# A fused sliding-attention and mixture-of-experts kernel: values of key blocks accumulated unsplit in two overlapping parts, loads moved, two router steps rewritten

## The chip, the cores and the metric

The kernel runs on one core of one Trainium2 chip. The metric is device time in microseconds (us) of one execution. A core has five engines that run side by side and wait for each other through semaphores: TensorE (PE in the profile; PEld is its weight load), VectorE (DVE), ScalarE (ACT), GpSimd (POOL) and SyncE (SP, which here only starts DMAs). Each engine runs its own instructions in program order. Matmuls write into PSUM, which VectorE and ScalarE read.

## What is computed

First causal attention with a window of 128 positions and a linear distance bias, then a router that gives each token to one of eight experts:

```
q, k, v: (8, 8, 576, 64)            # batch, heads, positions, head dimension
scores = q @ k.T / sqrt(64) - slope[h] * |i - j|,  kept where 0 <= i - j < 128
attn   = exp(scores - max); attn /= sum(attn)
x      = (attn @ v) as (4608 tokens, 512)
logits = x @ w_gate                  # (4608, 8)
e(t)   = argmax(logits); gate = softmax(logits)[e(t)]
out[t] = gate * (relu(x[t] @ w1[e(t)]) @ w2[e(t)])     # 512 -> 1024 -> 512
```

All is in float32.

## The kernel before

**Attention in 16 units.** A unit is a pair of batches and a pair of heads (four pairs of batches `bp`, four pairs of heads `hp`). Its 576 keys are nine blocks `kb` of 64 (`KB`). Key block `kb` is seen by 192 queries, from query 64·kb on (128 for block 7, 64 for block 8). A unit has four steps g = 0 to 3, one for a group of key blocks: (0, 1), (2, 3), (4, 5), (6, 7, 8). A step does, in this order, which is written out by hand in the loop at L1173:

- `load_unit` (L612): DMAs for k, q and half of v on SP, and for the other half of v on POOL, two units ahead;
- `scores(i + 2)` (L732): matmuls of keys and queries for the group two steps ahead (L739), the exponential on ScalarE (L745), and the multiplication with the bias and the mask on VectorE (L748, L753) into a tile `pe`;
- `values` (L762): matmuls of `pe` and `v` into the PSUM tile `at` (L774). Four 64x64 matmuls (two batches `c`, two heads `r`) occupy the four quadrants of the array at the same time;
- `finish` (L782) after a half of the queries: the eviction of `at` into `xT` on ScalarE (L791, L793), the sums of `pe` over keys by matmuls with a column of ones (L806) into a PSUM tile `m`, and their eviction into `sumT` (ScalarE L815 for the first head pair, else an addition on VectorE L817);
- `some()` (L1161): one entry of a list `tasks`, the router's work for the pair of batches before (`behind`, L1143).

The queries are cut into two halves (`QH`, L577): 0 to 319 and 320 to 575. Key blocks 3 and 4 are seen from both halves, so their matmuls are split. `at` is one tile of two PSUM banks with one buffer; each half uses it afresh. The PSUM tiles `m` share a pool of two buffers, for the sums and for all the router's matmuls.

**The router's tasks** are, by name: `gate`, `turn` (matmuls and turns of the logits), `scale_a` and `scale_b` (VectorE: the denominators, the logits summed over heads at L882, the best expert), `scale_c`, `count`, `place` (a token's place in its expert's list), `ones_at` (one-hot matrices `oc`, nine instructions at L955, and `orow`, L960), `enlist` (matmuls of both, L970), and `row` (a token tile turned by four matmuls, L984, evicted by ScalarE, L986, and written to memory). For batch pairs 0 to 2 they run in the steps of the next units; for the last pair they run as `with_tail` (L1426) between the matmuls of the first expert (L1273, L1330).

**Experts.** From about 190 us on TensorE runs eight experts, each with gathered rows (L1090) and scattered results (L1353).

The step that the change touches, for g = 2 and 3 (L1195 to L1204):

```
            elif g == 2:
                values(u, 0, (4,))
                finish(u, 0)
                values(u, 1, (3, 4, 5))
            else:
                values(u, 1, (6, 7, 8))
                finish(u, 1)
            ...
            some()
```

Of the kernel before, what the change touches and what calls it, by code (L numbers as in the profile page):

```python
# [457 lines left out]
def kernel(  # L458
# [12 lines left out]
    nc = tc.nc  # L471

    Dm, N = qT.shape
    D = Dm // H
    E = moe_w_gate.shape[1]
# [5 lines left out]
    KB = P // 2  # L481
    NK = S // KB
    BP = N // S // 2
    TPB = 2 * S // P
# [7 lines left out]
    NS = NJ + NF  # L492
# [13 lines left out]
    with ExitStack() as fast:  # L506
        def pool(stack, name, bufs, **kw):
            return stack.enter_context(tc.tile_pool(name=name, bufs=bufs, **kw))
# [65 lines left out]
              [(6, 0, 192), (7, 192, 128), (8, 320, 64)]]  # L574
        GC = 384
        LQ = 4 * P
        QH = [(0, 5 * KB), (5 * KB, 4 * KB)]  # L577

        ac = pool(att, "att_consts", 1)
        qk = pool(att, "qk", 3)  # L580
# [3 lines left out]
        ps_a = pool(att, "ps_a", 1, space=PSUM)  # L584
# [4 lines left out]
        units = [(bp, hp) for bp in range(BP) for hp in range(HP)]  # L589
# [58 lines left out]
        fac = ac.tile([P, H, GC], F32, name="fac")  # L648
# [8 lines left out]
        ind = ac.tile([P, HP, 32], F32, name="ind")  # L657
# [4 lines left out]
        none = ac.tile([P, 32], F32, name="none")  # L662
# [27 lines left out]
        K = {}  # L690
# [38 lines left out]
        prob, xT, sumT, gs = {}, {}, {}, {}  # L729
        at = {}  # L730
# [25 lines left out]
        def block(u, kb):  # L756

            g = min(kb // 2, 3)
            c0, n = next((c, n) for k, c, n in GR[g] if k == kb)
            return prob[4 * u + g], c0, n  # L760

        def values(u, half, kbs):  # L762

            bp, hp = units[u]
            q0, qn = QH[half]
            if (u, half) not in at:
                at[u, half] = ps_a.tile([P, 2, 512], F32, name="at"), set()
            acc, begun = at[u, half]
            for kb in kbs:
                pe, c0, n = block(u, kb)  # L770
                lo, hi = max(q0, kb * KB), min(q0 + qn, kb * KB + n)
                for c in range(2):
                    for r in range(2):
                        nc.tensor.matmul(  # L774
                            acc[r * D : (r + 1) * D, c, lo - q0 : hi - q0],
                            lhsT=v_sb[u][c * KB : (c + 1) * KB, kb, r * D : (r + 1) * D],
                            rhs=pe[c * KB : (c + 1) * KB, r, c0 + lo - kb * KB : c0 + hi - kb * KB],
                            start=(c, r) not in begun, stop=True, skip_group_check=True,
                        )
                        begun.add((c, r))  # L780

        def finish(u, half):  # L782

            bp, hp = units[u]
            q0, qn = QH[half]
            if hp == 0 and half == 0:
                xT[bp] = xp.tile([P, HP, 2 * S], F32, name="xT")
                sumT[bp] = xp.tile([P, S], F32, name="sumT")
            acc = at.pop((u, half))[0]
            n = min(q0 + qn, LQ) - q0  # L790
            nc.scalar.copy(xT[bp][:, hp, : 2 * LQ].rearrange("p (b q) -> p b q", b=2)[:, :, q0 : q0 + n], acc[:, :, :n])  # L791
# [3 lines left out]
            ops = []  # L795
            for kb in range(max(0, q0 // KB - 2), (q0 + qn) // KB):
                pe, c0, n = block(u, kb)
                lo, hi = max(q0, kb * KB), min(q0 + qn, kb * KB + n)
                ops.append((kb % 2, lo, hi, pe, c0 - kb * KB))
            if half == 0:  # L800
                ops.insert(0, (1, 0, KB, None, 0))
            begun = set()
            for par, lo, hi, pe, off in ops:
                for r in range(2):
                    j = 2 * r + par
                    nc.tensor.matmul(  # L806
                        sm[32 * j : 32 * j + 32, lo - q0 : hi - q0],
                        lhsT=none[:] if pe is None else ind[:, hp, :],
                        rhs=fac[:, 0, :KB] if pe is None else pe[:, r, off + lo : off + hi],
                        start=j not in begun, stop=True, skip_group_check=True,  # L810
                    )
                    begun.add(j)
            to = sumT[bp][:, q0 : q0 + qn]
            if hp == 0:
                nc.scalar.copy(to, sm[:, :qn])  # L815
            else:
                nc.vector.tensor_tensor(to, sm[:, :qn], to, op=ALU.add)  # L817


        def gate(bp, c):  # L820
# [58 lines left out]

        def scale_b(bp):  # L880
            lg = small.tile([P, TPB, E], F32, name="lg")
            nc.vector.reduce_sum(lg[:], pr_of[bp].rearrange("p t a h e -> p t e (a h)"), axis=AX)  # L882
# [67 lines left out]
        def ones_at(bp):  # L950

            rc = slot_of[bp]
            oc = small.tile([P, TPB, E * NS], F32, name="oc")
            for t in range(TPB):
                nc.vector.tensor_scalar(  # L955
                    oc[:, t, :], K["cols"][:, : E * NS], scalar1=rc[:, 1, t : t + 1],
                    scalar2=K["tok"][:, bp * TPB + t : bp * TPB + t + 1], op0=ALU.is_equal, op1=ALU.mult,
                )
            orow = small.tile([P, TPB, P], F32, name="orow")
            nc.vector.tensor_tensor(  # L960
                orow[:], K["cols"][:, None, :].to_broadcast([P, TPB, P]),
                rc[:, 0, :].unsqueeze(2).to_broadcast([P, TPB, P]), op=ALU.is_equal,
            )
            oh_of[bp] = oc, orow
# [196 lines left out]
        def some():  # L1161
            if tasks:
                for f in tasks.pop(0):
                    f()
# [8 lines left out]
        for i in range(NG):  # L1173
            u, g = divmod(i, 4)
            bp, hp = units[u]
            if g == (0 if u else 2) and u + 2 < len(units):
                load_unit(u + 2)
            if g == 0:
                if u == 5:
                    load_w1(fixed[0], w1_a)  # L1180
                if u == 1:
                    token_numbers()
                if u == 3:
                    table_consts()
            if i + AHEAD < NG:
                scores(i + AHEAD)
            if 8 <= u < 12 and g % 2 == 1:
                ws_tasks.pop(0)()
            if g == 0:
                values(u, 0, (0, 1))  # L1190
                if u < HP - 1:
                    factors(u + 1)
            elif g == 1:
                values(u, 0, (2, 3))
            elif g == 2:  # L1195
                values(u, 0, (4,))
# [250 lines left out]
        for i in range(len(groups)):  # L1447
            g = groups[i]
# [65 lines left out]
```

## Time and profile before

| | |
|---|---|
| median of 6 runs | 720.49 us (718.09 to 722.1) |
| the profiled execution | 719.96 us, of which its span from the first to the last instruction 718.1 us |
| TensorE busy | 682.4 us, 95% of the span |
| VectorE, ScalarE, GpSimd busy | 346.0, 225.4 and 136.4 us |
| granted TensorE clock, mean | 0.99 |

Matmuls are pipelined and their ends are modelled, so TensorE's busy share does not say that it runs at its peak. A row of the timeline holds: start in us, duration in us, engine, line, operation, tiles written and read, shape, count, and in brackets the idle time of the engine before it with what ended it. Every float32 matmul of the program appears as two records.

### The profile page before, as it was taken

The numbers are of one execution on the slowest core, as the hardware profiler recorded it, in microseconds if no ns is written. First come the engines' busy times: TensorE is split into PE (matmuls) and PEld (weight loads), VectorE is DVE, ScalarE is ACT, GpSimd is POOL, SyncE is SP. The second block draws the span as 40 slices with busy tenths as digits, with TensorE's granted clock in tenths as the row PEclk, the third lists the DMA queues.
The fourth block names the chain that finished last, engine by engine and source line by source line (L and its number), as shares of the span: only waits on it lengthen the run. The fifth ranks groups of instructions, "written<-read, shape, count | busy, mean of one in ns | idle before, by whom it ended". The sixth has DMA issues, their size and how long they took to land.

```text
span 718.1 us, 14588 instructions
## 1 busy us (share of the span) xinstructions
PE 682.4 (95%) x6204; PEld 568.9 (79%) x6204; DVE 346.0 (48%) x671; ACT 225.4 (31%) x410; POOL 136.4 (19%) x222
## 2 busy tenths in 40 slices
PE   5799999989899999999999999999999999999994
PEld 4587778667587888878897888888788978878892
DVE  3356748775558574433542535255145534433410
ACT  4455556454343223203311320232133023203200
POOL 4320133411100250023022002301220230021020
PEclk9999999999998999999999999999999999999998
DMA  9967885783515862185338236731843582184010
GB/s 253 242 203 247 238 239 182 206 224 98 175 72 185 293 241 66 53 291 209 118 94 314 89 118 210 283 118 36 291 171 118 170 307 76 57 290 150 1 59 8
DMA packets 52092, 122.00 MB, mean 170 GB/s; under 512 B 3680, under 2 KB 14528, under 8 KB 52017
## 3 DMA queue, kind: packets, MB, share of 16 engines
q1 hardware_dynamic: 43120, 95.66, 40.7%
q0 software_dynamic: 7744, 24.43, 10.3%
q8 instruction: 51, 0.84, 0.5%
q10 hardware_dynamic: 1152, 0.88, 0.4%
q14 instruction: 25, 0.20, 0.1%
HBM read 101.79 MB, written 19.96 MB: 170 GB/s over the span
## 4 chain that ended last, share of the span: by engine, by line
issue 57%; PE 21%; POOL 11%; DVE 4%; ACT 3%; DMA 3%; another core or an unknown queue 0%; POOLq 0%; DVEq 0%
PE sp L739 5%; POOL out_dram L1353 5%; PE at L774 5%; POOL xg L1090 5%; PE m L984 2%; PE m L806 2%; DMA v_sb<-in_v_dram 2%; PE m L970 1%; PE pair0b L1273 1%; ACT pe L745 1%; PE m L826 1%; ACT xT L791 1%; DMA out_dram<-zo,s_idx 1%; DVE pe L748 1%; DVE oc L955 1%
## 5 line engine op out<-in xcount | busy, mean ns | idle before, releaser
L1353 POOL DMA_INDIRECT out_dram<-zo,s_idx x39 | 43.9, 1125 | 384.5 <-DVE zo L1344 283.7
L774 PE MATMUL at<-pe,v_sb 64*64 64x192 f32 (+2 forms) x1408 | 63.0, 287 | 10.0 <-ACT xT L791 7.0
L748 DVE TENSOR_TENSOR pe<-pe,fac 128x768 f32<-128x768 f32 x48 | 46.1, 960 | 47.0 <-ACT pe L745 47.0
L739 PE MATMUL sp<-q_sb,k_sb 64*64 64x192 f32 (+2 forms) x1152 | 60.6, 322 | 8.1 <-DMA q_sb<-in_qT_dram 7.2
L745 ACT ACTIVATE pe<-sp 128x768 f32<-128x768 f32 x64 | 51.9, 812 | 50.9 <-PE sp L739 45.9
L774 PEld LDWEIGHTS at<-pe,v_sb 64*64 64x64 f32 x1408 | 47.8, 136 | 17.0 <-ACT xT L791 9.2
L739 PEld LDWEIGHTS sp<-q_sb,k_sb 64*64 64x64 f32 x1152 | 41.9, 137 | 20.4 <-issue 9.1
L1090 POOL DMA_INDIRECT xg<-x_rows,g_idx x39 | 42.9, 1101 | 31.5 <-DVE tb L1013 14.4
L1108 ACT COPY xgT<-m 128x512 f32<-128x512 f32 x39 | 22.9, 586 | 36.4 <-PE m L1107 35.4
L806 PE MATMUL m<-pe,ind 128*32 128x192 f32 (+2 forms) x704 | 30.4, 288 | 3.8 <-issue 3.4
L1284 ACT ACTIVATE h<-h 128x512 f32<-128x512 f32 x32 | 20.2, 630 | 40.3 <-DVE h L1283 35.1
L986 ACT COPY xs<-m 128x512 f32<-128x512 f32 x36 | 20.4, 585 | 31.9 <-PE m L984 17.0
L501 DVE TENSOR_TENSOR xn<-xg 128x512 f32<-128x512 f32 x39 | 26.1, 685 | 7.7 <-PE m L1107 7.7
L990 POOL COPY xs<-ext 128x16 f32<-128x16 f32 x36 | 13.8, 396 | 78.5 <-DVE ext L909 31.9
L806 PEld LDWEIGHTS m<-pe,ind 128*32 128x32 f32 x704 | 23.5, 110 | 6.6 <-issue 4.0
L608 POOL DMA_DIRECT2D v_sb<-in_v_dram x15 | 11.2, 747 | 77.3 <-PE at L774 75.6
L1107 PE MATMUL m<-ident,xn 128*128 128x128 f32 x156 | 23.5, 274 | 0.7 <-DVE xn L501 0.7
L1107 PEld LDWEIGHTS m<-ident,xn 128*128 128x128 f32 x156 | 19.2, 141 | 4.9 <-PE m L1107 0.9
L984 PE MATMUL m<-ident,xT 128*128 128x128 f32 x144 | 21.6, 281 | 0.5 <-DVE hole L1021 0.5
L1385 PE MATMUL pair2a<-w,h 128*128 128x512 f32 x48 | 21.1, 592 | 0.0
L753 DVE TENSOR_TENSOR pe<-pe,fac 128x768 f32<-128x768 f32 x16 | 15.2, 951 | 8.9 <-ACT pe L745 8.8
L791 ACT COPY xT<-at 128x640 f32<-128x640 f32 (+1 forms) x32 | 18.6, 581 | 2.2 <-PE m L806 1.3
(357 smaller groups left out, 1395.8 us busy)
## 6 DMA issues: line engine op xcount, KB each, us to landing
w<-in_moe_w_dram SPq DMA_DIRECT2D x30, 2048.0 KB, 10.0
k_sb<-in_kT_dram SPq DMA_DIRECT2D x15, 576.0 KB, 6.9
q_sb<-in_qT_dram SPq DMA_DIRECT2D x15, 576.0 KB, 7.8
x_rows<-xs SPq DMA_DIRECT2D x32, 264.0 KB, 2.9
v_sb<-in_v_dram SPq DMA_DIRECT2D x15, 288.0 KB, 6.8
v_sb<-in_v_dram POOLq DMA_DIRECT2D x15, 288.0 KB
x_rows<-xs SPq DMA_DIRECT2D x8, 132.0 KB, 2.4
xg<-x_rows,g_idx POOLq DMA_INDIRECT x39
```

The lines of the kernel that those rows point to most:

```text
L501: nc.vector.tensor_tensor(to.rearrange("p (h d) -> p h d", h=H), rows[:, :Dm].rearrange("p (h d) -> p h d", h=H), rows[:, Dm : Dm + H].uns ...
L739: nc.tensor.matmul(sp[c * KB : (c + 1) * KB, r, c0 : c0 + n], lhsT=k_sb[u][hs, c, kb * KB : (kb + 1) * KB], rhs=q_sb[u][hs, c, kb * KB : k ...
L745: nc.scalar.activation(pe[:], sp[:, :, :GC], AF.Exp, scale=SCALE)
L748: nc.vector.tensor_tensor(pe.rearrange("p r (k c) -> p r k c", k=2), pe.rearrange("p r (k c) -> p r k c", k=2), fac[:, h0 : h0 + 2, None, ...
L774: nc.tensor.matmul(acc[r * D : (r + 1) * D, c, lo - q0 : hi - q0], lhsT=v_sb[u][c * KB : (c + 1) * KB, kb, r * D : (r + 1) * D], rhs=pe[c ...
L791: nc.scalar.copy(xT[bp][:, hp, : 2 * LQ].rearrange("p (b q) -> p b q", b=2)[:, :, q0 : q0 + n], acc[:, :, :n])
L806: nc.tensor.matmul(sm[32 * j : 32 * j + 32, lo - q0 : hi - q0], lhsT=none[:] if pe is None else ind[:, hp, :], rhs=fac[:, 0, :KB] if pe is ...
L984: nc.tensor.transpose(ps[:, hp * P : (hp + 1) * P], xT[bp][:, hp, t * P : (t + 1) * P], ident[:])
L1090: nc.gpsimd.indirect_dma_start(out=g["xg"][:, j, :], out_offset=None, in_=src, in_offset=bass.IndirectOffsetOnAxis(ap=g_idx[:, g["c0"] + j ...
L1107: nc.tensor.transpose(tp[:, db * P : (db + 1) * P], xn[:, db * P : (db + 1) * P], ident[:])
L1108: nc.scalar.copy(g["xT"][:, :, j * P : (j + 1) * P], tp.rearrange("p (d q) -> p d q", d=DB))
L1353: ins = nc.gpsimd.indirect_dma_start(out=out[:, :], out_offset=bass.IndirectOffsetOnAxis(ap=s_idx[:, g["c0"] + j : g["c0"] + j + 1], axis= ...
```

## The change

Values: the two parts of the queries now overlap. Part 0 takes key blocks 0 to 4 whole (queries 0 to 447), part 1 key blocks 5 to 8 (queries 320 to 575). Queries 320 to 447 get a share from each: ScalarE evicts part 0 as it is, and VectorE adds part 1's share to it when it reads part 1. `at` becomes two tiles of one bank each, one for each batch. The sums are cut in the same way. The matmuls of key block 5 go behind `some()`.

Loads: units 2 and 3 (the third and the fourth) are loaded from unit 1's steps 0 and 2 instead of unit 0's step 2 and unit 1's step 0. Router: the logits' sum over eight heads is made by three additions instead of one reduction, and `oc` by two instructions over nine tiles instead of nine. Core of the diff:

```diff
-        QH = [(0, 5 * KB), (5 * KB, 4 * KB)]
+        QH = [(0, 5, 0, 7 * KB), (5, 4, 5 * KB, 4 * KB)]
...
 # values
-                at[u, half] = ps_a.tile([P, 2, 512], F32, name="at"), set()
+                at[u, half] = [ps_a.tile([P, 512], F32, name=f"at{c}") for c in range(2)], set()
...
-                lo, hi = max(q0, kb * KB), min(q0 + qn, kb * KB + n)
+                lo = kb * KB - q0
...
 # finish
-            n = min(q0 + qn, LQ) - q0
-            nc.scalar.copy(xT[bp][:, hp, : 2 * LQ].rearrange("p (b q) -> p b q", b=2)[:, :, q0 : q0 + n], acc[:, :, :n])
-            if n < qn:
-                nc.scalar.copy(xT[bp][:, hp, 2 * LQ :].rearrange("p (b q) -> p b q", b=2), acc[:, :, n:qn])
+            both = QH[1][2]
+            seen = QH[0][3]
+            for c in range(2):
+                x = xT[bp][:, hp, c * LQ : (c + 1) * LQ]
+                if half == 0:
+                    nc.scalar.copy(x[:, :seen], acc[c][:, :seen])
+                else:
+                    nc.vector.tensor_tensor(x[:, both:seen], acc[c][:, : seen - both], x[:, both:seen], op=ALU.add)
+                    nc.scalar.copy(x[:, seen:], acc[c][:, seen - both : LQ - both])
+                    nc.scalar.copy(xT[bp][:, hp, 2 * LQ + c * KB : 2 * LQ + (c + 1) * KB], acc[c][:, LQ - both : qn])
...
+            if half == 0:
+                add_up(
+                    1, lambda s: s.rearrange("p (a c) -> p a c", c=KB)[:, 0:7:6, :], none[:],
+                    lambda r: fac[:, r, : 2 * KB].rearrange("p (a c) -> p a c", c=KB),
+                )
+            else:
+                add_up(0, lambda s: s[:, :KB], none[:], lambda r: fac[:, r, :KB])
+            for kb in range(kb0, kb0 + kbn):
+                pe, c0, n = block(u, kb)
+                lo = kb * KB - q0
+                add_up(kb % 2, lambda s: s[:, lo : lo + n], ind[:, hp, :], lambda r: pe[:, r, c0 : c0 + n])
...
-            if hp == 0:
-                nc.scalar.copy(to, sm[:, :qn])
-            else:
-                nc.vector.tensor_tensor(to, sm[:, :qn], to, op=ALU.add)
+            add = qn if hp else (seen - both if half else 0)
+            if add:
+                nc.vector.tensor_tensor(to[:, :add], sm[:, :add], to[:, :add], op=ALU.add)
+            if add < qn:
+                nc.scalar.copy(to[:, add:], sm[:, add:qn])
...
 # scale_b
-            nc.vector.reduce_sum(lg[:], pr_of[bp].rearrange("p t a h e -> p t e (a h)"), axis=AX)
+            pr = pr_of[bp]
+            ph = pr[:, :, 0, :, :]
+            nc.vector.tensor_tensor(ph, ph, pr[:, :, 1, :, :], op=ALU.add)
+            nc.vector.tensor_tensor(ph[:, :, 0:2, :], ph[:, :, 0:2, :], ph[:, :, 2:4, :], op=ALU.add)
+            nc.vector.tensor_tensor(lg[:], ph[:, :, 0, :], ph[:, :, 1, :], op=ALU.add)
...
 # ones_at
-            for t in range(TPB):
-                nc.vector.tensor_scalar(
-                    oc[:, t, :], K["cols"][:, : E * NS], scalar1=rc[:, 1, t : t + 1],
-                    scalar2=K["tok"][:, bp * TPB + t : bp * TPB + t + 1], op0=ALU.is_equal, op1=ALU.mult,
-                )
+            nc.vector.tensor_tensor(
+                oc[:], K["cols"][:, None, : E * NS].to_broadcast([P, TPB, E * NS]),
+                rc[:, 1, :].unsqueeze(2).to_broadcast([P, TPB, E * NS]), op=ALU.is_equal,
+            )
+            nc.vector.tensor_tensor(
+                oc[:], oc[:],
+                K["tok"][:, bp * TPB : (bp + 1) * TPB].unsqueeze(2).to_broadcast([P, TPB, E * NS]), op=ALU.mult,
+            )
...
 # the loop over steps
-            if g == (0 if u else 2) and u + 2 < len(units):
+            if g == 0 and u == 1:
+                load_unit(2)
+            if g == (2 if u == 1 else 0) and 0 < u < len(units) - 2:
                 load_unit(u + 2)
...
                 values(u, 0, (4,))
                 finish(u, 0)
-                values(u, 1, (3, 4, 5))
...
             some()
+            if g == 2:
+                values(u, 1, (5,))
```

More of the change, by code (lines that the diff above doesn't have):

```diff
@@ L764, in values @@
             bp, hp = units[u]
-            q0, qn = QH[half]
+            q0 = QH[half][2]
             if (u, half) not in at:
-                at[u, half] = ps_a.tile([P, 2, 512], F32, name="at"), set()
+                at[u, half] = [ps_a.tile([P, 512], F32, name=f"at{c}") for c in range(2)], set()
             acc, begun = at[u, half]
@@ L774, in values @@
                         nc.tensor.matmul(
-                            acc[r * D : (r + 1) * D, c, lo - q0 : hi - q0],
+                            acc[c][r * D : (r + 1) * D, lo : lo + n],
                             lhsT=v_sb[u][c * KB : (c + 1) * KB, kb, r * D : (r + 1) * D],
-                            rhs=pe[c * KB : (c + 1) * KB, r, c0 + lo - kb * KB : c0 + hi - kb * KB],
+                            rhs=pe[c * KB : (c + 1) * KB, r, c0 : c0 + n],
                             start=(c, r) not in begun, stop=True, skip_group_check=True,
@@ L784, in finish @@
             bp, hp = units[u]
-            q0, qn = QH[half]
+            kb0, kbn, q0, qn = QH[half]
             if hp == 0 and half == 0:
@@ L789, in finish, with add_up @@
             acc = at.pop((u, half))[0]
-            n = min(q0 + qn, LQ) - q0
-            nc.scalar.copy(xT[bp][:, hp, : 2 * LQ].rearrange("p (b q) -> p b q", b=2)[:, :, q0 : q0 + n], acc[:, :, :n])
-            if n < qn:
-                nc.scalar.copy(xT[bp][:, hp, 2 * LQ :].rearrange("p (b q) -> p b q", b=2), acc[:, :, n:qn])
-            sm = ps_m.tile([P, 512], F32, name="m")
[L795 to L801, printed above, removed]
+            both = QH[1][2]
[8 more added lines that the diff above has]
+                    nc.scalar.copy(xT[bp][:, hp, 2 * LQ + c * KB : 2 * LQ + (c + 1) * KB], acc[c][:, LQ - both : qn])
+            sm = ps_m.tile([P, 512], F32, name="m")
             begun = set()
-            for par, lo, hi, pe, off in ops:
+            def add_up(par, to, lhsT, rhs):
                 for r in range(2):
@@ L806, in finish @@
                     nc.tensor.matmul(
[L807 to L810, printed above, removed]
+                        to(sm[32 * j : 32 * j + 32, :]), lhsT=lhsT, rhs=rhs(r), start=j not in begun, stop=True,
+                        skip_group_check=True,
                     )
                     begun.add(j)
-            to = sumT[bp][:, q0 : q0 + qn]
-            if hp == 0:
-                nc.scalar.copy(to, sm[:, :qn])
-            else:
-                nc.vector.tensor_tensor(to, sm[:, :qn], to, op=ALU.add)
+            if half == 0:
[9 more added lines that the diff above has]
+                add_up(kb % 2, lambda s: s[:, lo : lo + n], ind[:, hp, :], lambda r: pe[:, r, c0 : c0 + n])
+            to = sumT[bp][:, q0 : q0 + qn]
+            add = qn if hp else (seen - both if half else 0)
[3 more added lines that the diff above has]
+                nc.scalar.copy(to[:, add:], sm[:, add:qn])
         def gate(bp, c):
```

## The prediction, made before the change was run

> **What bounds the kernel now.** I read the page first. Its busy shares name one engine:
>
> ```profile
> PE 682.4 (95%) x6204; PEld 568.9 (79%) x6204; DVE 346.0 (48%) x671; ACT 225.4 (31%) x410; POOL 136.4 (19%) x222
> ```
>
> TensorE is the path. From about 190 us on it runs the experts, which the change does not touch, so what counts is each stretch before in which TensorE stands still, and its work there. The list of waits names the one that the change aims at:
>
> ```profile
> PE at L774 <- ACT xT L791: 7.0, 14, 0.5
> ```
>
> In 14 of 16 units the second half's values wait 0.5 us for ScalarE to empty `at`. The timeline of unit 9 shows that wait and, 4 us later, the place that decides this prediction:
>
> ```profile
> 111.89 0.69 ACT L791 COPY xT<-at 128x640 f32<-128x640 f32 x1
> ...
> 112.63 0.89 PE L774 MATMUL at<-pe,v_sb 64*64 64x64 f32 x24 [0.50 <-ACT xT L791]
> ...
> 114.52 1.22 DVE L882 TENSOR_REDUCE lg<-pr 128x72 f32<-128x576 f32 x1
> ...
> 116.83 0.83 PE L774 MATMUL at<-pe,v_sb 64*64 64x192 f32 x16
> ...
> 117.13 0.95 DVE L748 TENSOR_TENSOR pe<-pe,fac 128x768 f32<-128x768 f32 x1
> ...
> 118.00 0.42 DVE L817 TENSOR_TENSOR sumT<-m,sumT 128x256 f32<-128x256 f32 x1
> ```
>
> At 116.83 TensorE starts unit 10's values in an `at` that ScalarE had emptied at 115.6. VectorE is late there: it has just finished `scale_b` and multiplies step 3's probabilities only until 118.08.
>
> **Values and sums on TensorE: about 0.** In the timeline 16 records of 192 columns take 0.65 us to the next group; on four quadrants that is 768 columns in a row, 0.85 ns each. Unsplit or split, the columns are the same, so the 16 records that a unit saves are worth nothing here; step 1 and step 2 before `finish` get longer (+0.11 and +0.21 us) and step 2 after it shorter (-0.33). In the sums the fullest column group of part 0 grows from 448 to 576 columns, of part 1 shrinks from 384 to 320: with two records each, +0.21 and -0.11 us a unit. The first lies beside the eviction.
>
> **The wait in step 2, unit 9's case.** Evicting 640 columns takes 687 ns, 384 take 474 (0.83 ns a column), so each 448 takes 0.53, and the second starts 0.41 after the first. ScalarE starts them right after its exponential, as now: the second bank is free 0.25 us later than `at` is today. But TensorE then has only key block 5 to do (0.33 against 0.71 with its switch), and resumes the scores at 113.3 instead of 113.34. Where nothing of TensorE stands in `some()`, that is no gain: units 1, 2, 3, 5, 9, 12, 14. Where a token tile is turned there (0.59 us), it now covers the wait: units 7 and 11 gain 0.6 each. In units 6, 10 and 13 the turned tile needs the `m` buffer that `sumT`'s addition frees; VectorE multiplies until 1.1 us after the values' eviction starts and then adds 448 columns (0.61, from 484 ns for 320 and 420 for 256). I take +0.2 for units 6 and 10, 0 for 13; in units 4 and 8 `turn` waits for the same buffer, 0. Ends: all 14 waits go (-7.0 in all) or none (0).
>
> **The new wait in step 3.** Part 1 is now read by VectorE first. In the instruction list of the changed program the two additions stand right behind step 3's multiplication, and ScalarE's short copies wait for VectorE; behind them on ScalarE waits the next exponential, behind the next unit's values on TensorE all its scores. From the multiplication's end M: an addition of 128 columns from PSUM takes 0.29 (`gs` at L833), the second starts 0.21 later, so they end at M+0.21 and M+0.42 (engines overlap by 0.08). A copy of 64 columns is in no row; 128 columns take 0.28, so at most that, at least 0.12 (the spacing on ScalarE); I take 0.22. The banks are free at about M+0.6 and M+0.86. I read M and the start of the next values for each unit:
>
> - Units 5 and 9: M is 73.48 and 118.08, the values want to start at 72.1 and 116.8. The second bank comes at 118.95, values end at 119.6 instead of 117.5: +2.0 each.
> - Units 2, 3, 12, 14: M lies 0.2 before to 0.4 before the start (50.69 against 50.90): +0.6 each. Unit 10: +0.35.
> - Units 4, 6, 7, 8, 11, 13: 0.7 to 3.5 us between, covered: 0. Units 0, 1: the values of units 1 and 2 wait for `v` or pause anyway (0.24 and 1.4 us in the timeline), 0.
> - Unit 13's `place` waits for VectorE today (1.4 us); three more instructions of VectorE stand before it in step 3 of unit 12, less the shorter `scale_b`: +0.4.
>
> Ends: 0.2 (if VectorE came first everywhere, only switches remain) and 10 us (every unit 0.6).
>
> One rule speaks against this part. The Trainium skill, "PSUM — Partial Sum Buffer", section on bank collisions, has two engines' accesses to one bank kept apart, reads against reads too; no run here shows it, since ScalarE alone reads `at` today. Without it the copies would not stand behind the additions, each tight unit would cost 0.44 less, and the sum would be 3 us lower.
>
> **Router.** `oc`: nine instructions take 1.93 us at 219.24 (spaced 0.21) and 3.2 in unit 11 beside GpSimd. Two of 432 elements: 512 elements take 0.69, spaced 0.60, so 0.6 each, 1.2 together; the bounds are 1.0 and 1.9. In unit 11 TensorE waits 0.39 + 0.5 for the multiplication behind `oc`; that goes: -0.85. In unit 7 no TensorE wait hangs on it: 0. `lg`: 1.22 becomes 288, 144 and 72 elements, by L875 (0.42 for 288) and L887 (0.23 for 72) 0.45 + 0.31 + 0.25 = 1.0: -0.2, which the longer `sumT` addition (+0.13) eats; that is in M above.
>
> **The tail.** Here `oc` is on the path:
>
> ```profile
> 219.24 2.02 DVE L955 TENSOR_SCALAR oc<-cols,rc,tok 128x48 f32<-128x48 f32 x9
> ...
> 221.17 1.35 DVE L960 TENSOR_TENSOR orow<-cols,rc 128x1152 f32<-128x1152 f32 x1
> ...
> 224.31 3.16 PE L970 MATMUL m<-oc,orow 128*128 128x48 f32 x18 [1.39 <-DVE hs L529]
> ```
>
> `orow`, an addition to `h`, its relu and the eviction of `xs` follow in a chain, and the matmuls of `enlist` wait for them: 0.75 us earlier, -0.75. After that stop the clock drops (us, busy times, then the granted clock before the DMA share):
>
> ```profile
> 222.00:227.00 5.00, 3.61 (x22) 3.16 (x21) 3.62 (x6) 2.09 (x4) 0.00 (x0) 0.84 0.35 101
> 227.00:232.00 5.00, 5.00 (x14) 4.10 (x14) 4.22 (x8) 0.60 (x1) 0.00 (x0) 0.50 0.98 320
> ```
>
> 6.8 us at half clock cost 3.4. If the stop halves, the dip may go: 0 to -3.4. The stop between 153.7 and 157.1, where TensorE was active for some 1.3 us of 3.4, kept the clock; the shorter stop comes nearer to that, so I take -2.2. The Trainium skill, "TensorE: Matmul & The Clock Gate", Part 1, gates after a whole idle window of about 3.4 us. The row differs: 1.4 us idle and sparse matmuls sufficed. By the rule alone no stop here would cost any clock.
>
> **Loads.** SP issues the same DMAs in the same order; none waits on where the loop calls it. On POOL `v` of unit 3 moves behind the 40 iotas and their neighbours (3.87 + 0.6 + 0.6 us). It was issued at 18.79 after waiting for unit 0's values; the iotas now fill that wait. `v` is needed at 43: 0, and 0 even if it comes 5 us later. No gain either, since no byte moves.
>
> **Sum.** -0.6 - 0.6 - 0.85 + 4.0 + 2.4 + 0.35 + 0.4 + 0.4 = +5.5 in attention, -0.75 - 2.2 in the tail: +2.55. The profiled execution took 719.96 (span 718.1 and 1.86 around), so 722.5; it lies 0.53 under the median of the runs shown, 720.49, so I predict **723.0**.
>
> **Rivals.** About 0.3% (2.2 us) is what a measurement of this kernel can tell from no change.
>
> - *VectorE drains earlier.* Units 5 and 9 wait only 0.5 each, because `scale_b`'s chain ends sooner: 723.0 - 3.0 = 720.0. For it: the tree is shorter. Against: VectorE is busy without a gap from 112.38 to 118.4, and 0.2 us is all that leaves it.
> - *The eviction is covered everywhere* (the other side): the 14 waits of step 2 go, since block 5 stands behind `some()` and is short; I counted 1.2 of 7.0, so 5.8 more: 717.2. It makes the kernel faster by over 0.3% once 4.7 of the 5.8 go. Against it: in seven units there is nothing of TensorE between.
> - *The new waits cost clock too*: two stops of 2 us each trip it once for 3.4 us at half clock, twice over: 723.0 + 3.4 = 726.4. For it: the tail's dip followed a stop of 1.4 us. Against: the sparse `enlist` matmuls helped there.
> - Pauses that TensorE shows as "issue" (3.19 us at 24.5, 0.8 at 74) may move with the instruction count: up to 3 us either way, in the range.
>
> **How the numbers follow.** Forecast 0.50, of which 0.16 lies within 0.3%; drained early 0.18 (0.12 within, 0.06 below); covered 0.22 (0.20 faster); clock 0.10, slower. So faster 0.26, same 0.30, slower 0.44. The likeliest case alone spans 721 to 725.5. For 8 in 10 the range goes from 717.8, the covered case, to 726.4, the clock case.
>
> **What would show it.** Right: the waits list names TensorE at L776's values waiting for ScalarE's short copies, about 2 us in units 5 and 9; `oc` near 0.6 us an instruction; the dip at 225 us shorter or gone. Wrong: no such wait at the start of units 6 and 10, or TensorE's second wait in step 2 gone in the units without tasks. The whole fails if the pauses named "issue" change by more than 3 us.

## The result and the profile after

The changed kernel takes 722.65 us (median of 37 runs, 720.01 to 726.14), the kernel before 719.49 in the same comparison (74 runs): a ratio of 1.0043, interval 1.0033 to 1.0052. It is slower by 3.1 us. A second comparison, on a single chip (e9 below), gives 720.82 against 715.15, ratio 1.0088 (1.0059 to 1.0117); both are used below. The profiled execution after has a span of 718.7 us, against 718.1.

The engines' row of the page:

```profile
PE 684.9 (95%) x5884; PEld 565.0 (79%) x5884; DVE 350.1 (49%) x687; ACT 227.7 (32%) x458; POOL 133.4 (19%) x222
```

TensorE has 320 records fewer and is busy 2.5 us longer: unsplit key blocks save records, not time. The 14 waits of TensorE for the eviction in step 2 have left its list (its weight loads still wait, 0.30 and 0.23 us in unit 9). The new entries, ScalarE's first and then two of TensorE's (view filtered to that engine; columns: total us, times, longest):

```profile
ACT xT L800 <- DVE xT L799: 23.5, 16, 3.1
```

```profile
PE at L776 <- ACT xT L801: 4.7, 6, 1.7
PE m L865 <- ACT sumT L832: 3.2, 4, 1.0
```

The first two are the chain that the prediction described: VectorE adds first, ScalarE's short copies wait, TensorE's values wait for them. The third, the router's `turn`, stands in no term of the prediction for step 3. The timeline of unit 9, where VectorE is late (`lg` is now three instructions):

```profile
115.48 0.45 DVE L899 TENSOR_TENSOR pr<-pr 128x288 f32<-128x288 f32 x1
...
115.96 0.31 DVE L900 TENSOR_TENSOR pr<-pr 128x144 f32<-128x144 f32 x1
...
116.30 0.23 DVE L901 TENSOR_TENSOR lg<-pr 128x72 f32<-128x72 f32 x1
...
117.93 0.95 DVE L750 TENSOR_TENSOR pe<-pe,fac 128x768 f32<-128x768 f32 x1
118.80 0.48 DVE L799 TENSOR_TENSOR xT<-at,xT 128x128 f32<-128x128 f32 x2
119.12 0.21 ACT L800 COPY xT<-at 128x64 f32<-128x64 f32 x1 [3.06 <-DVE xT L799]
...
119.50 1.78 PE L776 MATMUL at<-pe,v_sb 64*64 64x192 f32 x16 [1.64 <-ACT xT L801]
```

The multiplication ends at 118.88, the additions 0.40 later, the copies at 119.67; TensorE stood still for 1.64 us, until the first bank's copies were done. The windows of that stop and of what follows (length, busy time and count of TensorE, its weight loads, VectorE, ScalarE and GpSimd, then the granted clock, the DMA share and GB/s):

```profile
117.90:119.60 1.70, 0.10 (x2) 0.11 (x4) 1.70 (x5) 0.48 (x5) 0.00 (x0) 0.99 1.16 263
119.60:123.00 3.40, 3.40 (x52) 3.17 (x56) 1.95 (x7) 1.75 (x5) 0.14 (x2) 0.50 0.07 11
```

So this execution ran 3.4 us at half clock here. In the tail `oc` takes 1.24 us instead of 2.02, `enlist` waits 0.62 us instead of 1.39, and the clock stays:

```profile
222.64 0.60 DVE L973 TENSOR_TENSOR oc<-cols,rc 128x432 f32<-128x432 f32 x1
...
223.27 0.61 DVE L977 TENSOR_TENSOR oc<-oc,tok 128x432 f32<-128x432 f32 x1
...
226.94 2.21 PE L992 MATMUL m<-oc,orow 128*128 128x48 f32 x18 [0.62 <-ACT xs L1008]
```

```profile
224.70:229.70 5.00, 4.38 (x29) 3.78 (x28) 4.06 (x8) 2.09 (x4) 0.00 (x0) 1.00 0.36 102
229.70:234.70 5.00, 5.00 (x27) 4.45 (x26) 4.83 (x14) 1.23 (x3) 0.00 (x0) 1.00 0.96 325
```

Against the profile before, the first expert's matmuls start 3.4 us later and the span ends only 0.6 later. The third entry of the waits belongs to `turn` in units 4 and 8, here unit 4:

```profile
59.89 0.48 DVE L799 TENSOR_TENSOR xT<-at,xT 128x128 f32<-128x128 f32 x2
...
60.63 0.31 ACT L832 COPY sumT<-m 128x128 f32<-128x128 f32 x1
...
60.99 0.33 PE L865 MATMUL m<-ident,gs 128*128 128x128 f32 x1 [1.02 <-ACT sumT L832]
```

`turn` needs the `m` buffer that the copy of `sumT` frees; that copy stands on ScalarE behind the short copies, and those behind VectorE's additions.

**Time lost by unit.** The start of a unit's first values is a mark on TensorE. The difference of a mark between a kernel and the profile before, less the same for the next mark, is what the kernel loses (+) or gains in that unit, in us. All of the table is worked out from the profiles; the kernels to the right are the experiments below. A star marks a unit in which TensorE had 3.41 us at half clock (in unit 10 that costs 0.7 us: 1.80 against 1.10 in e9).

| unit | predicted | changed | again (e9) | values only (e3) | no additions (e4) | order mended (e12) | scratch (e10) |
|---|---|---|---|---|---|---|---|
| 3 | +0.6 | 0.80 | 0.76 | 0.76 | 0.19 | 0.19 | 0.19 |
| 4 | 0 | 1.24 | 1.24 | 1.24 | 0.45 | 0.77 | 0.85 |
| 5 | +2.0 | 1.82 | 1.81 | 1.96 | -0.07 | 0.95 | -0.08 |
| 6 | +0.2 | -0.49 | -0.49 | -0.49 | -0.68 | -0.49 | -0.41 |
| 7 | -0.6 | -0.39 | -0.39 | -0.04 | -0.64 | -0.65 | -0.65 |
| 8 | 0 | 0.97 | 0.97 | 0.97 | 0.45 | 0.97 | 3.84* |
| 9 | +2.0 | 1.75 | 1.75 | 1.90 | -0.08 | 0.88 | 0.66 |
| 10 | +0.55 | 1.80* | 1.10 | 1.10 | -0.03 | 1.10 | 0.84 |
| 11 | -1.45 | -1.24 | -1.25 | -0.47 | -1.23 | -1.23 | -1.10 |
| 12 | +0.6 | 0.32 | 0.32 | 0.32 | -0.08 | -0.08 | -0.08 |
| sum | +3.9 | 6.6 | 5.8 | 7.3 | -1.7 | 2.4 | 4.1 |

Where kernels share the code, units 3 to 12 repeat within 0.2 us but for single pauses and dips (e1 and e2 have some of 0.4 to 3 us in units 8 to 10); units 0 to 2 do not repeat (the start of unit 3's values lies between 41.9 and 43.5 in five runs with the old values, between 39.5 and 42.9 in nine with the new ones).

### The profile page after: what moved, and what is told of

Read it like the earlier page. It is cut to its first block, busy times and chain, and to the rows that moved or that the text cites. A ratio compares the mean times of both kernels' runs of the same rounds, so it can differ in the third digit from the quotient of the medians.

```text
span 718.7 us, 14005 instructions
## 1 busy us (share of the span) xinstructions
PE 684.9 (95%) x5884; PEld 565.0 (79%) x5884; DVE 350.1 (49%) x687; ACT 227.7 (32%) x458; POOL 133.4 (19%) x222
## 4 chain that ended last, share of the span: by engine, by line
issue 55%; PE 21%; POOL 9%; DVE 8%; ACT 3%; DMA 3%; another core or an unknown queue 0%; POOLq 0%; SPq 0%; ACTq 0%; DVEq 0%
POOL out_dram L1378 5%; PE at L776 5%; PE sp L741 5%; POOL xg L1112 4%; DVE pe L750 2%; PE m L1006 2%; PE m L810 2%; ACT pe L747 2%; DMA q_sb<-in_qT_dram 2%; PE m L992 1%; DMA xg<-x_rows,g_idx 1%; PE m L841 1%; PE pair0b L1298 1%; PE pair0a L1298 1%; PE pair2a L1298 0%
## 5 line engine op out<-in xcount | busy, mean ns | idle before, releaser
L776 PE MATMUL at<-pe,v_sb 64*64 64x192 f32 (+2 forms) x1152 | 70.3, 319 | 7.3 <-ACT xT L801 4.7
L741 PE MATMUL sp<-q_sb,k_sb 64*64 64x192 f32 (+2 forms) x1152 | 63.7, 326 | 7.0 <-DMA q_sb<-in_qT_dram 6.2
L741 PEld LDWEIGHTS sp<-q_sb,k_sb 64*64 64x64 f32 x1152 | 45.3, 139 | 20.4 <-issue 8.2
L1309 ACT ACTIVATE h<-h 128x512 f32<-128x512 f32 x32 | 20.2, 630 | 39.5 <-DVE h L1308 35.4
L1012 POOL COPY xs<-ext 128x16 f32<-128x16 f32 x36 | 11.4, 329 | 83.8 <-DVE ext L928 33.1
L810 PEld LDWEIGHTS m<-pe,ind 128*32 128x32 f32 x576 | 22.0, 111 | 0.2
L1006 PEld LDWEIGHTS m<-ident,xT 128*128 128x128 f32 x144 | 16.0, 143 | 6.7 <-DVE sumT L830 2.1
```

Of the source, the lines that this page charges most:

```text
L741: nc.tensor.matmul(sp[c * KB : (c + 1) * KB, r, c0 : c0 + n], lhsT=k_sb[u][hs, c, kb * KB : (kb + 1) * KB], rhs=q_sb[u][hs, c, kb * KB : k ...
L776: nc.tensor.matmul(acc[c][r * D : (r + 1) * D, lo : lo + n], lhsT=v_sb[u][c * KB : (c + 1) * KB, kb, r * D : (r + 1) * D], rhs=pe[c * KB : ...
L810: nc.tensor.matmul(to(sm[32 * j : 32 * j + 32, :]), lhsT=lhsT, rhs=rhs(r), start=j not in begun, stop=True, skip_group_check=True,)
L1006: nc.tensor.transpose(ps[:, hp * P : (hp + 1) * P], xT[bp][:, hp, t * P : (t + 1) * P], ident[:])
```

## The experiments

Theory: the new wait in step 3 (VectorE before ScalarE before TensorE) is what the change costs; the unsplit values, the step-2 wait and the loads are worth little; the router's part gains. Rivals: the loads made the early gain of 3 us in the profile; the additions are not the cause, but the more numerous copies; pauses and clock dips move by themselves.

### e1: the router's two edits alone

```diff
 # the kernel before
-            nc.vector.reduce_sum(lg[:], pr_of[bp].rearrange("p t a h e -> p t e (a h)"), axis=AX)
+            nc.vector.tensor_tensor(ph, ph, pr[:, :, 1, :, :], op=ALU.add)
...
-            for t in range(TPB):
-                nc.vector.tensor_scalar(
...
+            nc.vector.tensor_tensor(
+                oc[:], K["cols"][:, None, : E * NS].to_broadcast([P, TPB, E * NS]),
...
```

> The kernel before with the two router edits alone (logits as a tree, oc in two instructions). My theory: unit 11 loses its wait behind oc (-0.85 us); in the tail oc is 0.9 us shorter and stands on the path (-0.9), and the clock dip of 6.8 us at half clock behind it goes (-3.4): 719.5 - 5.1 = 714.4 us. Rival, the dip left the changed kernel's tail because its attention ended 3.4 us later: the dip stays here, 717.7 us.

713.80 against 715.72 us, ratio 0.9977 (0.9954 to 1.0): -1.65 us, with an interval from -3.3 to 0. Unit 11 gains 0.89, and `enlist` waits 0.62 instead of 1.39, as in the changed kernel: together -1.66. Yet the clock dips here as well, behind the shorter stop:

```profile
223.14 2.21 PE L977 MATMUL m<-oc,orow 128*128 128x48 f32 x18 [0.62 <-ACT xs L993]
```

```profile
221.80:226.80 5.00, 4.38 (x26) 3.65 (x25) 4.06 (x9) 2.09 (x4) 0.00 (x0) 0.86 0.54 125
226.80:231.80 5.00, 5.00 (x20) 4.23 (x19) 4.72 (x14) 0.97 (x2) 0.59 (x1) 0.80 0.96 378
```

The rival is nearer in size: the router is worth about 1.65 us, and no dip more.

### e2: the loads alone

```diff
 # the kernel before
-            if g == (0 if u else 2) and u + 2 < len(units):
+            if g == 0 and u == 1:
+                load_unit(2)
+            if g == (2 if u == 1 else 0) and 0 < u < len(units) - 2:
                 load_unit(u + 2)
```

> The kernel before with the loads of units 2 and 3 one unit (half a unit) later, and nothing else. My theory: no transfer is late, 0: 719.5 us. Rival: the 3 us that the changed kernel gains in units 0 to 2 come from the moved loads (fewer transfers beside the fetch of the instructions): 716.5 us, with the pause of 3.2 us at 24.5 shorter and the one of 1.4 us at 33.4 gone.

716.30 against 715.72, ratio 1.0006 (0.9986 to 1.0026). No change beyond 0.3%, as predicted; the pauses ahead of the sums (3.15 us at 24.2) and at 32.3 (2.02) are there.

### e3: values unsplit alone

```diff
 # the changed kernel
-            if g == 0 and u == 1:
-                load_unit(2)
-            if g == (2 if u == 1 else 0) and 0 < u < len(units) - 2:
+            if g == (0 if u else 2) and u + 2 < len(units):
                 load_unit(u + 2)
...
+            nc.vector.reduce_sum(lg[:], pr_of[bp].rearrange("p t a h e -> p t e (a h)"), axis=AX)
...
+            for t in range(TPB):
+                nc.vector.tensor_scalar(
...
```

> The changed kernel with the router and the loads as before: values unsplit alone. My theory: attention +3.4 us as in the changed kernel, and 0.85 more because oc in unit 11 is as before; the tail as before: 719.5 + 4.2 = 723.7 us. Rival, the gain of 3 us in units 0 to 2 is that of the loads: 726.7 us. Rival, the second half's wait for the eviction, which goes from step 2, is worth more than the new wait costs: under 719.5.

722.96 against 715.72, ratio 1.0106 (1.0073 to 1.0139): +7.6 us, 3 above what I expected. The rival of the loads has the size and not the mechanism: unit 3's values start 2.9 us earlier than in the profile before here too, without the moved loads. My 4.2 came from one pair of profiles, and the one before was long in units 14 and 15 (e8). Units 3 to 12 lose 7.3 us. The parts add up: 1.0106 times 0.9977 is 1.008.

### e4: without VectorE's additions

```diff
 # the changed kernel
-                    nc.vector.tensor_tensor(x[:, both:seen], acc[c][:, : seen - both], x[:, both:seen], op=ALU.add)
```

> The changed kernel without VectorE's two additions in each unit: what key blocks 5 to 8 give to queries 320 to 447 is left out of x. ScalarE then reads part 1's banks without standing behind VectorE. My theory, this new wait is what costs the changed kernel its time: units 3, 4, 5, 8, 9, 10 and 12 get back 0.6 to 1.8 us each, with the clock dip of unit 10: 722.6 - 6 = 716.6 us, and the values at L776 wait nowhere over 0.3 us in step 0. Rival, ScalarE's two short copies behind its exponential and the spacing of its instructions cost most of it: 721 us.

With the share left out, the router fills other lists, and the experts' stage of this run (2114.74 us in all) says nothing. Its attention does: in the table units 3 to 12 gain 1.7 us instead of losing 5.8, 7.5 us for two additions a unit. TensorE's values wait for ScalarE's copies nowhere any more. Units 5 and 9 give back 1.9 and 1.8, units 10, 4, 3, 8 and 12 0.4 to 1.1. The theory holds: the same copies on ScalarE, without VectorE ahead of them, are waited for no longer. What is left in units 4 and 8, 0.45, is `turn`, since VectorE still reads the sums in `m` before ScalarE copies the rest of them:

```profile
PE m L864 <- ACT sumT L831: 2.1, 4, 0.6
```

### e5: VectorE's additions ahead of the multiplication

```diff
 # the changed kernel, in step 3 alone
         def finish(u, half):
             ...
                     nc.vector.tensor_tensor(x[:, both:seen], ...)
             ...
+            if half and 4 * u + 5 < NG:
+                mask_late(4 * u + 5)      # the multiplication, taken out of scores(i + 2)
             sm = ps_m.tile([P, 512], F32, name="m")
```

> The changed kernel with VectorE's order turned in step 3 alone: its two additions stand ahead of the step's multiplication instead of behind it. My theory: the new wait comes from standing behind that multiplication (0.95 us, late by scale_b in units 5 and 9); about 0.9 us less in units 5 and 9, 0.3 to 1.1 less in units 3, 4, 8, 10 and 12, and no new wait, since the multiplied tile is read a step later: 5 us less than the changed kernel, 2 us under the kernel before (ratio 0.997). Rival, the additions only trade places: the late multiplication holds the next values or the next exponential as long: as the changed kernel, ratio 1.004.

720.67 against 715.02, ratio 1.0075 (1.0052 to 1.0098). Units 3, 5 and 9 gained 0.8 to 0.9 us each against the changed kernel, as the theory has it, but the time hardly moved. The timeline at the end of unit 8 shows what took it back:

```profile
104.81 0.49 DVE L809 TENSOR_TENSOR xT<-at,xT 128x128 f32<-128x128 f32 x2 [2.71 <-PE at L786]
105.06 0.76 POOL L610 DMA_DIRECT2D v_sb<-in_v_dram  x1 [6.95 <-PE at L786]
...
105.22 3.93 DVE L763 TENSOR_TENSOR pe<-pe,fac 128x768 f32<-128x768 f32 x1
...
105.83 1.28 POOL L531 TENSOR_TENSOR w<-w 128x512 f32<-128x512 f32 x1
107.05 1.27 POOL L532 TENSOR_TENSOR ws<-w,ws 128x512 f32<-128x512 f32 x1
...
109.70 0.47 PE L877 MATMUL m<-ident,gs 128*128 128x128 f32 x1 [3.72 <-ACT sumT L844]
```

A multiplication of 0.95 us took 3.93: it started while GpSimd issued the DMA of `v` and ended 0.83 after GpSimd's second sum (108.32). Once more, at 132.63, one took 4.20. The DMA waits for the end of a unit's values, as the additions do. In the changed kernel the multiplication starts 0.04 us ahead of the same DMA (105.66 against 105.70) and takes 0.96; here it starts 0.16 behind it. The DMA alone does not hold it: in six other units of this run the multiplication starts as soon after the DMA's start, no sum of GpSimd follows, and it takes 0.95 to 0.96. At 105.22, 132.63 and in e11 a sum follows 0.6 us after the multiplication's start, and all three were held.

### e6: key block 5 ahead of the router's task

```diff
 # the changed kernel
                 finish(u, 0)
+                values(u, 1, (5,))
...
             some()
-            if g == 2:
-                values(u, 1, (5,))
```

> The changed kernel with key block 5's values ahead of the step's router task again, as in the kernel before. My theory: a turned token tile no longer covers the eviction, so units 6, 7 and 11 lose 0.4 to 0.6 each, the others nothing: +1.5 us against the changed kernel (ratio to the kernel before 1.006). Rival, the eviction of the first half is waited for nowhere in the changed kernel: then every unit loses 0.3 and more, +5 us (1.011). Rival, the order does not matter: 1.004.

719.65 against 715.02, ratio 1.0069 (1.0045 to 1.0093); its interval overlaps that of the changed kernel on the same chip (1.0088), so the time decides nothing. By the marks, units 7 and 11 lose 0.56 and 0.55 against the changed kernel, unit 6 gains 0.30, the others are the same: the turned tile covers the eviction in 7 and 11 only.

### e7: the kernel before, with the router's edits and the later order

```diff
 # e1
                 finish(u, 0)
-                values(u, 1, (3, 4, 5))
...
             some()
+            if g == 2:
+                values(u, 1, (3, 4, 5))
```

> The kernel before with the two router edits, and with the second half's values of step 2 (key blocks 3, 4, 5, still split) behind the router's task instead of ahead of it: what the change could have without the additions. My theory: units 6, 7 and 11 gain up to 0.6 each from the order, on top of the router's gain: 1.5 us less than the router edits alone, ratio to the kernel before 0.9955. Rival, the order brings nothing without the shorter key block 5: 0.9977, as the router edits alone.

714.97 against 715.02, ratio 0.9999 (0.9975 to 1.0022). The rival is nearer: unit 11 gains 0.49 against e1, unit 6 loses 0.41, since the turned tile now waits 0.99 us for its `m` buffer. Unit 7 loses 2.5 in this profile; a pause of 1.28 us without a named wait and a window of half clock lie in it, so it says nothing of the order. No gain from the order by itself can be shown.

### e8: the kernel before, profiled once more

```diff
 # no edit
```

> The kernel before, profiled once more, to see which pauses and clock dips stay in place from run to run. If the pauses of 3.2 us at 24.5 and 1.4 us at 33.4, the dip of 6.8 us at 225 and the stutter of units 14 and 15 (3.5 us) are properties of the kernel, they are here again. Rival, they move from run to run: then the 3 us that the changed kernel gains in units 0 to 2, and part of what the tail gives back, are not the change's.

The same stop of 1.39 us ahead of `enlist`, and no dip behind it:

```profile
221.54 2.21 PE L970 MATMUL m<-oc,orow 128*128 128x48 f32 x18 [1.39 <-ACT xs L986]
```

```profile
219.20:224.20 5.00, 3.61 (x26) 3.11 (x25) 4.06 (x8) 2.09 (x4) 0.00 (x0) 1.00 0.35 101
224.20:229.20 5.00, 5.00 (x27) 4.43 (x26) 4.86 (x13) 1.13 (x3) 0.00 (x0) 1.00 0.92 325
```

The dips stand at 34.6 and 157.5 instead of 27.4 and 225.4, and units 14 and 15, where the first profile shows TensorE halting every few matmuls, are 1.75 and 1.93 us shorter. So these are not fixed properties of the kernel. An early pause nearly is: in every profile but e9 one of 1.5 to 3.2 us starts between 23 and 26 us; e9 has 2.4 us at 32 instead.

### e9: the changed kernel once more

```diff
 # no edit to the changed kernel
```

> The changed kernel once more, beside the two kernels below on one chip, as their base. The parts measured so far add up: values alone 1.0106, router alone 0.9977, loads 1.0006, so 1.009 if they add; 1.0043 as measured before, if router and values overlap.

720.82 against 715.15, ratio 1.0088 (1.0059 to 1.0117): on this chip the parts add up. Units 3 to 12 repeat the first profile to 0.04 us but for the dip of unit 10; here the half clock is at 162.8, for 6.83 us.

### e10: through a scratch tile

```diff
 # the changed kernel, half 1
-                    nc.vector.tensor_tensor(x[:, both:seen], acc[c][:, : seen - both], x[:, both:seen], op=ALU.add)
+                    part = ep.tile([P, seen - both], F32, name=f"part{c}", bufs=2)
+                    nc.scalar.copy(part[:], acc[c][:, : seen - both])
+                    late.append((x[:, both:seen], part))
...
+            for x, part in late:
+                nc.vector.tensor_tensor(x, part[:], x, op=ALU.add)
```

> The changed kernel, but ScalarE first copies part 1's 128 overlapping queries of each bank into a scratch tile, and VectorE adds them to x from there. The same sums, but the banks wait for ScalarE alone. My theory, standing behind VectorE is the new wait: units 3, 4, 5, 8, 9, 10 and 12 get back 0.4 to 1.8 us each, some 6 us in all, less 0.2 for the longer eviction in tight units: 5.5 us under the changed kernel (ratio to the kernel before about 0.997), with no wait over 0.4 us ahead of the values of step 0. Rival, two more copies on ScalarE make the tight units as late as before: ratio as the changed kernel's.

718.43 against 715.15, ratio 1.0057 (1.003 to 1.0085): 2.4 us under the changed kernel, where I expected 5.5. The wait of the values is gone and units 5 and 9 give back 1.9 and 1.1. Unit 8 takes part of it back: two additions of 0.28 us took 2.70.

```profile
105.18 2.70 DVE L806 TENSOR_TENSOR xT<-part,xT 128x128 f32<-128x128 f32 x2
107.80 0.28 DVE L835 TENSOR_TENSOR sumT<-m,sumT 128x128 f32<-128x128 f32 x1
```

Their inputs are now both in SBUF, and GpSimd summed weights from 105.17 to 107.73. Read from PSUM, the same additions take 0.28 beside GpSimd. The `sumT` behind them came late, and `turn` waited 3.11 us.

### e11: the additions first, but in two units

```diff
 # e5
-            if half and 4 * u + 5 < NG:
+            if half and 4 * u + 5 < NG and u not in (8, 11):
                 mask_late(4 * u + 5)
...
 # scores
-            if g == 1:
+            if g == 1 and u not in (9, 12):
                 return
```

> VectorE's additions ahead of step 3's multiplication as in the run before, except in units 8 and 11, where the multiplication of 0.95 us took 3.9 and 4.2 us while GpSimd started a DMA and summed weights. My theory, the order saves 0.9 us a unit and these two stalls took it back: 3 to 5 us under the changed kernel of this call, with no multiplication over 2 us. Rival, the stalls move to other units (9 and 10): as the changed kernel.

716.68 against 715.15, ratio 1.0036 (1.0018 to 1.0054): 4.1 us under the changed kernel. But a multiplication of 4.20 us is still there, at 126.19: I had named the wrong unit. The second stall lies at the end of unit 10.

### e12: the exception in the right place

```diff
 # e11
-            if half and 4 * u + 5 < NG and u not in (8, 11):
+            if half and 4 * u + 5 < NG and u not in (8, 10):
                 mask_late(4 * u + 5)
...
 # scores
-            if g == 1 and u not in (9, 12):
+            if g == 1 and u not in (9, 11):
                 return
```

> As the run before, with the exception in the right place: the additions stand ahead of step 3's multiplication in all units but 8 and 10. The run before had kept the changed order in units 8 and 11, but its second stall (4.2 us instead of 0.95) was still there, at the end of unit 10. My theory, a multiplication that starts while GpSimd works is held until GpSimd pauses: no multiplication over 2.1 us, unit 11 gains 1.3 us against the run before (as in the changed kernel, -1.2 against the kernel before): ratio 1.0018. Rival, the stall has another cause and appears elsewhere: 1.0036 as the run before.

721.34 against 719.29 on another chip, ratio 1.002 (1.0005 to 1.0035), where 1.0018 was expected. No multiplication takes over 1.84 us, and unit 11 gains 1.23, where e11 loses 0.07. The rival's 1.0036 lies just outside the interval, so it is the marks that decide. Of the theory, the word "works" is too wide: beside a DMA issue alone no multiplication was held (e5). The values wait for the copies still in units 5 and 9, half as long:

```profile
PE at L786 <- ACT xT L811: 1.6, 2, 0.8
```

**The best version measured** is e1, the router's edits on the old values: 0.9977, interval 0.9954 to 1.0. Since the interval reaches 1.0, and e7, which holds the same edits, measured 0.9999, a gain over the kernel before is likely and not shown.

## Why the prediction was right, and where it was not

The forecast, 723.0 us and slower, came true with 722.65. Its main reason held; two of its terms were off in opposite directions. It also started from 720.49 us, 1.0 above the kernel before in the comparison: forecast were +2.55 us, measured +3.1.

- **Values and sums on TensorE, about 0: right.** 320 records less, and no time: e4 has the same matmuls, and its units 3, 5, 9, 10 and 12 stand within 0.2 us of the kernel before.
- **The new wait in step 3, the main term: right in mechanism.** That ScalarE's copies stand behind VectorE's additions, where the prediction had a doubt, is in the list: 16 waits, 23.5 us, by the order of the program; whether two engines could read one bank at once no run tried. For units 3 to 12 the term was 5.55 us (2.0 twice, 0.6 twice, 0.35), and e4 prices it at 7.5. Units 5 and 9 measured 1.9 and 1.8 (2.0 predicted). Mis-sized is the line "Units 4, 6, 7, 8, 11, 13: 0.7 to 3.5 us between, covered: 0". I looked there only at the next unit's values. In units 4 and 8 `turn` needs the buffer that ScalarE's copy of `sumT` frees, and that copy queues behind the short copies: 1.24 and 0.97. Of this 0.79 and 0.52 go with the additions (e4); the other 0.45 each stays without them, since VectorE and ScalarE now read the sums in `m` one after the other. The prediction names `turn` in step 2 alone, at 0. I had followed ScalarE's queue to the next exponential and left out `sumT`. In unit 10 it was the turned tile behind `place` in step 2, which waited 1.35 us for VectorE's sum (e9): 1.10, not 0.55, and not at the place where the 0.35 was expected.
- **The wait in step 2: nearly right.** Units 7 and 11 gain by the order (e6: 0.56 and 0.55, predicted 0.6 each). Unit 6 gained 0.49 where I took +0.2. In the units without tasks the waits went over to the weight loads, 0.30 and 0.23 for the two banks in unit 9, and TensorE was not earlier, as predicted (units 5, 9 and 12 of e4: 0.07 to 0.08). By its letter one sign of being wrong came true, TensorE's second wait is gone from its list; the gain that it stood for did not come.
- **Router: right.** `oc` 0.60 and 0.61 us an instruction, unit 11 -0.89 (predicted -0.85), tail -0.77 (-0.75), `lg` 1.05 from its first start to its last end (1.0). Unit 7, where I gave the router nothing, gains nothing by it on the old values (e1: +0.03) and 0.35 on the new ones (-0.39 against -0.04 without).
- **The clock dip, -2.2: wrong as a step, and it happened in the pair of profiles.** "If the stop halves, the dip may go": e8 keeps the stop and has no dip, e1 has the shorter stop and a dip. Over all profiles a dip follows the stop of 1.39 us in two of four (the kernel before and e2; not e3, e8) and the stop of 0.62 us in two of nine (e1 and e11): too few to show a gain, and on the mean less than 1 us where I took 2.2. The row that I leaned on reads otherwise, too: from 153.7 to 157.1 TensorE's matmuls were busy 1.91 us, its weight loads 1.37. The third rival, that the new waits cost clock, is not dead either: of the eight stops of 1.6 to 1.9 us at the ends of units 5 and 9 (the changed kernel, e3, e6, e9) two were followed by 3.41 us at half clock, both at the end of unit 9 (the changed kernel and e6), at some 0.7 us each.
- **Loads, 0: right** (e2).
- **Sum.** In truth attention costs more: 5.8 us in units 3 to 12 against the first profile (5.1 against e8), and by the marks some 0.1 to 0.3, 0.4 and 0.5 in units 13 to 15, so 6 to 7. The tail gives 0.8 and no clock that can be shown. That leaves +5 to +6; e9's ratio of 1.0088 is +6.3, its interval 4.2 to 8.4. I had +5.5 and -2.95. The number 723.0 owes part of its accuracy to the two errors cancelling, which is luck. The lower end of the range, 717.8, stands 0.6 above the case that it is said to be (717.2).
- **What stays open:** why the first comparison shows 1.0043 and e9 1.0088, with intervals that do not touch. Where the kernel before takes 719 to 720 us, the profile of it and that of e12 show TensorE halting in units 14 and 15 without a named wait (3.7 us for the kernel before, against the profile at 714.7). In the first changed profile unit 14 has no such halts and unit 15 has 2.4 us of them, which would account for 1.3 of the 3 us. What makes TensorE halt there, and whether the unsplit values, with fewer records, halt less, was not tried. The same holds for the early pause: with the new values unit 3 starts 1.1 us earlier on the mean (41.4 against 42.5), which a spread of up to 3.5 us does not make certain. Nor is it known why a multiplication that starts before GpSimd's sum, but during the DMA issue ahead of it, is held through both sums.

## What to carry to other kernels

An operation that joins two engines in the eviction of one buffer costs what stands ahead of it on the later engine, not its own 0.28 us; follow the queue behind it to its last instruction, since a copy far behind it (here `sumT`) can hold a buffer that a third party needs. Before an instruction is moved to the moment when a unit ends, look which GpSimd work waits for the same moment. A clock dip seen in one profile is no sure term of a sum: profile the same kernel several times and count.

## What the runs showed of the hardware

- **VectorE and GpSimd hold each other up by where VectorE's inputs lie.** In the thirteen profiles other than e4, and ahead of 190 us, every addition or multiplication on VectorE with two SBUF inputs that started while one of GpSimd's tensor sums had more than 0.2 us left (29 multiplications by the mask, 12 of `slot`, 3 from the scratch tile) took longer by the rest of that sum less 0.12 to 0.15 us: 0.95 us became 1.10 to 2.07, 0.23 became 0.71 to 1.35, 0.28 became 1.35 to 1.43. None of the 55 with an input in PSUM did (`xT` from `at` 0.28, `sumT` 0.28 to 0.48 by its length, `gs` 0.68, `cn` 0.15 to 0.17). The Trainium skill, "SBUF — State Buffer", section "SBUF: two separate sides", says this: the shared port pair is an exclusive lock, taken by an instruction with two SBUF inputs against a GpSimd operation that reads SBUF, and the second one waits. The numbers agree. Where the multiplication came first, the sum waited: in e5 one that started 0.02 us ahead of a sum took its 0.96, and the sum 2.08 instead of 1.28. The exception is a multiplication that starts during GpSimd's DMA issue with a sum right behind: three of three were held through two GpSimd sums on end, 3.0 to 3.2 us beyond their own 0.95. With no sum behind the issue, 18 of 18 in e5, e11 and e12 took 0.95 to 0.96.
- **The clock drops for whole windows.** Each of the dips in the first 240 us of these profiles lasts 3.41 or 6.83 us, and each begins in a stop of TensorE of 0.6 to 3.7 us or within 2.6 us behind it, but most such stops are followed by none. They come back at a few places, not in every run: at 26 to 29 us, in or behind the early pause, in eight of the fourteen profiles, at 157 to 164 us in seven. The Trainium skill, "TensorE: Matmul & The Clock Gate", Part 1, has a free-running window of about 3.4 us, which fits the lengths; its whole idle window is not needed here: in e1 a stop of 0.62 us, with 18 small matmuls in the 2.05 us behind it, was followed by 3.41 us at half clock.
